# Rounding the joined high word of a float64 weight before its low bits are added

## The chip, the cores and the metric

The kernel runs on one core of a Trainium2 chip. The time is the device time of one execution in microseconds (us). The engines go by the names of the profile: PE is TensorE (PEld its weight loads), DVE is VectorE, ACT is ScalarE, POOL is GpSimd, SP issues the DMAs.

## The reference, cut to what matters

```python
def _attn_ref(q, k, v, n_sink, window):          # q, k, v: 4 x 8 x 768 x 64, float32
    scores = scale * np.matmul(q, k.transpose(0, 1, 3, 2))
    keep = is_sink | in_window                    # 4 sinks, a window of 128
    scores = np.where(keep, scores, -1000000000.0)
    ...
    return np.matmul(a, v).astype(np.float32)

def _moe_ref(x, w_in, w_out, s, b):               # x: 3072 x 512, w_in: 512 x 2048, w_out: 2048 x 512
    h = x @ w_in
    r = np.maximum(h, 0.0)
    g = s * (r * r) + b
    return (g @ w_out).astype(np.float32)
```

The attention's output is the x of the second function. Two lines of the set-up decide this case: `w_in` and `w_out` are float32 draws times a NumPy float64 scalar, so both arrive as float64, 8 bytes a number. The chip's engines take them as pairs of 32-bit words.

## The kernel before, in words

**The work in the large.** The 3072 tokens are eight chunks of 384. Each chunk has an attention part and a two-layer part (in the code `moe_steps`): `l1(f)` multiplies the chunk with columns f of `w_in` (line 598, 12 matmuls of 384 columns), and `l2(f)` adds g times rows f of `w_out` into three accumulators (line 617, 9 matmuls of 512 columns), for f from 0 to 15, l2 two steps behind l1. While the two-layer part of chunk c runs, the attention of chunk c+1 is put between its steps. Chunks 0 and 1 have a plain attention (class `Plain`): scores on PE (line 500), mask and maximum on DVE (515), the exponential on ACT (517), the division on DVE (`norm`, lines 522, 523 and six multiplications at 528), transposes on PE (540), their copies on ACT (542), the product with v on PE (551), and the result split in two on ACT and DVE (553, 554).

**Two words a weight.** A matmul here multiplies rounded float32 (F32R). Every operand is therefore held as a rounded part and a remainder, and each product is made of three matmuls (rounded x rounded, rounded x remainder, remainder x rounded). Sixteen weights f have to be made from float64 in that way, each a tile of 128 x 1024 numbers, and this is done once, for chunk 0. The scores and transposes of chunk 1 run in the same stretch.

**How one weight f is made.** `load_weight(f)` brings the float64 pairs into the place of weight f+1 (the tile w{f+1}); `raw[..., 0]` is the low word of each number, `raw[..., 1]` the high one. `make_weight(j)` has three steps for a weight, at j = 2f, 2f+1 and 2f+2:

- 211, ACT: the low word is scaled down to the 3 bits that the high word lacks; 212, ACT: the high word, read as a float32, is scaled so that its exponent fits.
- 213, DVE: the high word is shifted left by 3 into a scratch tile `wt`; 214, DVE: sign and shifted bits are joined, into the high word.
- 216, POOL: the low bits are added as integers, and the sum goes into the high word.
- 220, ACT: the sum is rounded into F32R, piece 0 of weight f (tile w{f}).
- 225: sum minus rounded part, the remainder, into piece 1. POOL does it for odd f, DVE for even f.

The last three raws (f = 13, 14, 15) come in halves or quarters with the same steps.

**What sets the order.** The instructions of an engine run in the order of its queue. That order is made when the kernel is built, by a scheduler that sorts the instructions of the whole program by when it reckons them ready; the kernel's own text gives only the start of it (`before(f)` asks, ahead of l1(f), for loads up to f + 6 and for the steps up to j = 2f + 4). Waits are semaphores between engines. So a changed dependency also moves instructions on the engines that take part, and those on either side of them.

**The WAR side.** Since raw f lies in the place of weight f+1, line 220 for weight f+1 must wait until line 225 for weight f has read its raw.

Of the kernel before, what the change touches and what calls it, by code (L numbers as in the profile page):

```python
# [6 lines left out]
F32 = mybir.dt.float32  # L7
# [5 lines left out]
ALU = mybir.AluOpType  # L13
# [27 lines left out]
def tile_kernel(ctx, tc, qT, kT, k0, v, vsk, n_sink, window, w, s, b, out):  # L41
    nc = tc.nc
# [127 lines left out]
    def place(f):  # L170
        return (const if f < NEARLY else late[0]).tile([P, 2, 2, DM], F32, tag=f"w{f}", name=f"w{f}")
# [15 lines left out]
    def scratch(f, j):  # L187

        if len(raws[f]) == 1:
            tag = f"w{NF - 2 + f % 2}"  # L190
            return (late[0] if late else first).tile([P, 2, DM], I32, tag=tag, name="wt", bufs=1)
        return wk.tile([P, DM], I32, tag="ot", name="wt")[:, :raws[f][j].shape[1]]

    def piece(f, j, t):

        n = len(raws[f])
        if n == 1:
            return weight[f][:, :, t, :]
        a = DM * 2 // n
        return weight[f][:, j * 2 // n, t, j * a % DM:j * a % DM + a]  # L200

    def make_weight(j):

        f = j // 2
        if j % 2 == 0 and f < NF:
            for i, raw in enumerate(raws[f]):
                lo, hi = raw[..., 0], raw[..., 1]
                t = scratch(f, i)  # L210
                nc.scalar.activation(lo, lo.bitcast(U32), AF.Copy, scale=2.0 ** -29)
                nc.scalar.mul(hi.bitcast(F32), hi.bitcast(F32), 2.0 ** -111)
                nc.vector.tensor_scalar(out=t, in0=hi, scalar1=3, scalar2=None, op0=ALU.logical_shift_left)  # L213
                nc.vector.scalar_tensor_tensor(out=hi, in0=hi, scalar=-0x80000000, in1=t,  # L214
                                               op0=ALU.bitwise_and, op1=ALU.bitwise_or)
                nc.gpsimd.tensor_tensor(out=hi, in0=hi, in1=lo, op=ALU.add)  # L216
        if j % 2 == 1:
            weight[f] = place(f).bitcast(F32R)
            for c, raw in enumerate(raws[f]):
                nc.scalar.copy(piece(f, c, 0), raw[..., 1].bitcast(F32))  # L220
        f -= 1
        if j % 2 == 0 and f >= 0:
            for c, raw in enumerate(raws[f]):
                e = nc.gpsimd if f % 2 == 1 else nc.vector
                e.tensor_tensor(out=piece(f, c, 1), in0=raw[..., 1].bitcast(F32), in1=piece(f, c, 0).bitcast(F32), op=ALU.subtract)
            raws.pop(f)


# [491 lines left out]
    def weights(n_load, n_make):  # L720
        while made[0] < min(n_make, 2 * NF + 1):
            while made[0] // 2 >= loaded[0] and loaded[0] < NF:
                load_weight(loaded[0])
                loaded[0] += 1
            make_weight(made[0])
            made[0] += 1

        n_wide = NF - NARROW - 1
        while loaded[0] < min(n_load, NF) and (loaded[0] < n_wide or made[0] > 2 * n_wide - 2):
            load_weight(loaded[0])  # L730
            loaded[0] += 1
# [102 lines left out]
```

## Time and profile before

| | |
|---|---|
| median of 3 executions | 739.83 us (738.43 to 743.51) |
| the profiled execution, its own time | 739.34 us |
| its span in the trace | 737.2 us |
| mean granted TensorE clock | 0.977 of 2.4 GHz |
| busy: PE, DVE, ACT, POOL | 704.9, 516.1, 480.0, 396.3 us |

A row of a timeline has the start in us, the duration, the engine, the line, the operation, the output and input tiles with their shapes (partitions x elements), the count, and in brackets the idle time of the engine before it with what ended that. Durations of consecutive instructions on DVE and ACT overlap by some 0.1 us. A row of waits names who waited for whom, the total, the number of times and the longest. A row by windows has, for a stretch of the span, the busy time of each engine with its instructions, then the granted clock, the DMA engines' share and GB/s.

### The profile page before, as it was taken

What the parts mean: (1) busy time and instruction counts of PE and PEld (TensorE: products, weight loads), DVE (VectorE), ACT (ScalarE), POOL (GpSimd) and SP (SyncE); (2) the same over time, 40 slices, a digit from 0 to 9 for tenths busy, and PEclk for the clock granted to TensorE, in tenths of its full rate; (3) what the DMA queues carried; (4) which work ended last, traced back from release to release, by engine and by line L of the source; (5) the groups of instructions that cost most, each with busy time, mean ns of one, the idle gap of its engine ahead of it and who ended that gap; (6) DMA issues with size and microseconds to landing.
All of it is one profiled execution on the core that took longest, in us unless ns stands there. A gap on an engine that the chain in (4) does not pass through costs nothing.

```text
span 737.2 us, 11878 instructions
## 1 busy us (share of the span) xinstructions
PE 704.9 (96%) x3848; PEld 622.0 (84%) x3848; DVE 516.1 (70%) x1213; ACT 480.0 (65%) x1169; POOL 396.3 (54%) x641
## 2 busy tenths in 40 slices
PE   6788899899999999999999999999999999999996
PEld 3367677789988999999998999999999999989895
DVE  6779999738984788757785588847886589743331
ACT  5978888568774787656884677746775677633222
POOL 2254555348991689616773589816775389710000
PEclk9879989999999999999999999999999999999998
DMA  7844122041210212111121222111111212000001
GB/s 280 337 171 193 33 102 72 15 139 51 80 63 31 84 55 65 34 61 54 46 64 44 82 63 64 46 54 49 56 53 45 84 42 59 12 18 26 1 1 47
DMA packets 27221, 53.01 MB, mean 72 GB/s; under 512 B 3472, under 2 KB 15376, under 8 KB 25232
## 3 DMA queue, kind: packets, MB, share of 16 engines
q1 hardware_dynamic: 27152, 52.18, 21.2%
q8 instruction: 32, 0.52, 0.3%
q14 instruction: 37, 0.30, 0.1%
HBM read 45.88 MB, written 6.29 MB: 71 GB/s over the span
## 4 chain that ended last, share of the span: by engine, by line
PE 79%; DVE 10%; DMA 3%; ACT 3%; POOL 2%; issue 1%; SPq 1%; POOLq 0%; ACTq 0%; DVEq 0%
PE po L617 32%; PE h L598 32%; PE o L376 3%; PE sc L303 2%; PE sc L304 2%; PE sc L324 2%; DMA vf<-in_v 2%; DMA w<-in_w 2%; DVE w L214 2%; DVE g L606 1%; DVE wt L213 1%; PE ts L390 1%; POOL w L216 1%; DVE smf L528 1%; DVE r L603 1%
## 5 line engine op out<-in xcount | busy, mean ns | idle before, releaser
L598 PE MATMUL h<-x,w 128*128 128x384 f32 x1536 | 299.8, 344 | 1.1 <-ACT tf L542 0.8
L617 PE MATMUL po<-w,g 128*128 128x512 f32 x1152 | 298.0, 404 | 0.0
L598 PEld LDWEIGHTS h<-x,w 128*128 128x128 f32 x1536 | 268.6, 189 | 6.7 <-ACT tf L542 1.1
L617 PEld LDWEIGHTS po<-w,g 128*128 128x128 f32 x1152 | 212.4, 191 | 45.0 <-issue 2.7
L603 DVE SCALAR_TENSOR_TENSOR r<-h,sb,r 128x384 f32<-128x384 f32 x128 | 78.6, 614 | 82.5 <-ACT r L601 82.2
L606 DVE SCALAR_TENSOR_TENSOR g<-r,sb,g 128x384 fp32r<-128x384 f32 x128 | 102.0, 797 | 39.0 <-ACT g L605 38.2
L340 POOL TENSOR_TENSOR hl<-two,hl 128x256 fp32r<-128x256 f32 x128 | 99.3, 776 | 21.4 <-ACT hl L339 18.2
L601 ACT ACTIVATE r<-h 128x384 f32<-128x384 f32 x128 | 62.3, 487 | 66.7 <-PE h L598 66.5
L605 ACT ACTIVATE g<-r,sb 128x384 fp32r<-128x384 f32 x128 | 78.7, 615 | 34.1 <-DVE r L603 32.8
L317 POOL TENSOR_TENSOR sm<-sm 128x128 f32<-128x128 f32 x128 | 68.0, 531 | 59.5 <-ACT sm L314 55.5
L314 ACT ACTIVATE sm<-sm,negm 128x272 f32<-128x272 f32 (+1 forms) x144 | 73.1, 507 | 35.4 <-DVE negm L308 31.0
L308 DVE CUSTOM_DVE_ANT_0 sm<-sc,msk 128x272 f32<-128x272 f32 (+1 forms) x144 | 60.4, 419 | 40.4 <-PE sc L304 32.6
L284 POOL TENSOR_TENSOR kl<-kraw,kh 128x544 fp32r<-128x544 f32 (+1 forms) x48 | 63.1, 1315 | 21.7 <-ACT kh L282 21.7
L339 ACT CAST hl<-two 128x256 fp32r<-128x256 f32 x128 | 50.6, 395 | 31.6 <-DVE two L337 31.6
L216 POOL TENSOR_TENSOR w<-w 128x1024 int32<-128x1024 int32 (+1 forms) x17 | 32.6, 1919 | 45.6 <-DVE w L214 25.1
L337 DVE TENSOR_TENSOR two<-sc,split 128x256 f32<-128x256 f32 x128 | 53.0, 417 | 4.4 <-POOL hl L340 4.2
L318 POOL COPY psk<-sm 128x48 f32<-128x48 f32 x144 | 40.7, 282 | 26.7 <-ACT sm L314 26.1
L289 POOL TENSOR_TENSOR vv<-vraw,vv 128x256 fp32r<-128x256 f32 (+1 forms) x48 | 34.4, 718 | 24.6 <-ACT vv L288 24.6
L376 PE MATMUL o<-hl,vv 128*128 128x256 f32 (+1 forms) x256 | 44.5, 276 | 0.0
L303 PE MATMUL sc<-kh,qs 128*128 128x272 f32 (+1 forms) x144 | 42.6, 298 | 0.0
L376 PEld LDWEIGHTS o<-hl,vv 128*128 128x128 f32 x256 | 39.6, 189 | 2.9
L304 PE MATMUL sc<-kl,qs 128*128 128x272 f32 (+1 forms) x144 | 41.3, 288 | 0.0
(129 smaller groups left out, 904.4 us busy)
## 6 DMA issues: line engine op xcount, KB each, us to landing
w<-in_w SPq DMA_DIRECT2D x15, 1024.0 KB, 9.0
kraw<-in_kT SPq DMA_DIRECT2D x32, 272.0 KB, 2.6
out<-ot SPq DMA_DIRECT2D x24, 256.0 KB, 2.0
qraw<-in_qT SPq DMA_DIRECT2D x24, 192.0 KB, 2.4
vraw<-in_v SPq DMA_DIRECT2D x16, 256.0 KB, 2.7
kraw<-in_kT SPq DMA_DIRECT2D x16, 208.0 KB, 2.4
vsraw<-in_vsk SPq DMA_DIRECT2D x24, 64.0 KB, 2.0
vraw<-in_v SPq DMA_DIRECT2D x8, 192.0 KB, 2.4
```

Of the source, the lines that this page charges most:

```text
L284: nc.gpsimd.tensor_tensor(out=hd.kl[:, :kw], in0=hd.k[:, :kw], in1=hd.kh[:, :kw].bitcast(F32), op=ALU.subtract)
L308: nc.vector.tensor_tensor_reduce(out=sm[:, :n], in0=sc[:, :n], in1=m, scale=-0.125, scalar=BIG, op0=ALU.add, op1=ALU.min, accum_out=negm[: ...
L314: nc.scalar.activation(sm[:, :n], sm[:, :n], AF.Exp, bias=negm[:, uu], scale=-1.0, accum_out=pp.zz[:, i, hh:hh + 1])
L317: nc.gpsimd.tensor_tensor(out=sm[:, c1:c1 + P], in0=sm[:, p1:p1 + P], in1=sm[:, c1:c1 + P], op=ALU.add)
L340: nc.gpsimd.tensor_tensor(out=lo, in0=both, in1=hi.bitcast(F32), op=ALU.subtract)
L376: nc.tensor.matmul(hd.o[:, q0:q0 + n * P], hd.vv[:, kb, :], hd.hl[:, t, c0 * P:(c0 + n) * P], start=(hd.n == 0), stop=(i == BLK - 1 and kb ...
L598: nc.tensor.matmul(h[:, :CH], weight[f][:, 0, wi, cc * P:(cc + 1) * P], x[xi][:, cc, :], start=(i == 0), stop=(i == 11))
L601: nc.scalar.activation(r, h[:, :CH], AF.Relu, scale=1.0 / WUP)
L603: nc.vector.scalar_tensor_tensor(out=r, in0=h[:, :CH], scalar=sw_ap, in1=r, op0=ALU.mult, op1=ALU.mult)
L605: nc.scalar.activation(gg[:, 0, :], r, AF.Identity, bias=b_ap, scale=1.0)
L606: nc.vector.scalar_tensor_tensor(out=gg[:, 1, :], in0=r, scalar=b_ap, in1=gg[:, 0, :].bitcast(F32), op0=ALU.add, op1=ALU.subtract)
L617: nc.tensor.matmul(po[tb], gg[:, gi, tsl], weight[f][:, 1, wi, :], start=(f == 0 and i == 0), stop=(f == NF - 1 and i == 2))
```

## The change

The integer addition on POOL puts its sum into the low word instead of the high one, so that the high word stays as DVE joined it. ACT's rounding (line 220, not touched in the text) then reads the high word without the low bits, and the remainder (line 225) is taken from the sum in the low word. The rounded part can so be made of a number whose three lowest bits are zero; rounded part plus remainder is the sum, as before.

```diff
-                nc.gpsimd.tensor_tensor(out=hi, in0=hi, in1=lo, op=ALU.add)
+                nc.gpsimd.tensor_tensor(out=lo, in0=hi, in1=lo, op=ALU.add)
...
-                e.tensor_tensor(out=piece(f, c, 1), in0=raw[..., 1].bitcast(F32), in1=piece(f, c, 0).bitcast(F32), op=ALU.subtract)
+                e.tensor_tensor(out=piece(f, c, 1), in0=raw[..., 0].bitcast(F32), in1=piece(f, c, 0).bitcast(F32), op=ALU.subtract)
```

Line 220 depended on 216 and now depends on 214. Line 225 depended on 220 and now depends on 220 and 216. The numbers and sizes of the instructions stay. PE's queue changes in 13 rows out of 2459 (one score matmul earlier), POOL's in 10 rows at the end of the stretch, SP's not at all. DVE's and ACT's queues change through the whole stretch in which weights are made.

On DVE, at the middle of the stretch (trace of before: 79 to 95 us). In these names w9_604 is the raw of weight 8 in the place of weight 9, w8_828 is weight 8, w10_651 the raw of weight 9; sc is a bank of scores, smf their exponentials, zf the divisors, g and r belong to l1.

```order
 L213 TENSOR_SCALAR wt_774<-w9_604 128x1024
-L214 SCALAR_TENSOR_TENSOR w9_604<-w9_604,wt_774 128x1024
 L606 SCALAR_TENSOR_TENSOR g_738<-r_735,sb_72,g_738 128x384
 L515 ISA smf_766,negm_102<-sc_762,m_all_70 128x384
 L515 ISA negm_102 128x1
+L214 SCALAR_TENSOR_TENSOR w9_604<-w9_604,wt_774 128x1024
 L515 ISA smf_769,negm_102<-sc_764,m_all_70 128x384
 L515 ISA negm_102 128x1
-L213 TENSOR_SCALAR wt_830<-w10_651 128x1024
-L214 SCALAR_TENSOR_TENSOR w10_651<-w10_651,wt_830 128x1024
+L225 TENSOR_TENSOR w8_828<-w9_604,w8_828 128x2x512
 L603 SCALAR_TENSOR_TENSOR r_796<-h_783,sb_72,r_796 128x384
```

The join of raw 8 stands two scores later than before, the remainder of weight 8 stands right behind the last score, and the two DVE steps of raw 9 have moved behind it.

On DVE, at the end of the stretch (trace of before: 127 to 132 us). w15_1013 is the raw of weight 14 in halves, w14_1193 is weight 14, the wraw tiles are the quarters of raw 15.

```order
 L214 SCALAR_TENSOR_TENSOR wraw_1015<-wraw_1015,wt_1196 128x256
 L214 SCALAR_TENSOR_TENSOR wraw_1017<-wraw_1017,wt_1202 128x256
+L225 TENSOR_TENSOR w14_1193<-w15_1013,w14_1193 128x512 x2
 L213 TENSOR_SCALAR wt_1208<-wraw_1019 128x256
-L225 TENSOR_TENSOR w14_1193<-w15_1013,w14_1193 128x512
+L213 TENSOR_SCALAR wt_1214<-wraw_1021 128x256
 L214 SCALAR_TENSOR_TENSOR wraw_1019<-wraw_1019,wt_1208 128x256
-L225 TENSOR_TENSOR w14_1193<-w15_1013,w14_1193 128x512
-L213 TENSOR_SCALAR wt_1214<-wraw_1021 128x256
 L214 SCALAR_TENSOR_TENSOR wraw_1021<-wraw_1021,wt_1214 128x256
```

Both remainders of weight 14 now stand ahead of the last two quarters of raw 15.

On ACT, near 64 us of the trace of before. w5_642 is weight 5, w6_402 its raw, g_622 and r_666 belong to l1(3) and l1(4), w8_552 is raw 7, w6_711 weight 6.

```order
 L212 ACTIVATE w7_404<-w7_404 128x1024
+L220 CAST w5_642<-w6_402 128x2x512
+L605 ACTIVATE g_622<-r_619,sb_72 128x384
 L211 ACTIVATE w8_552<-w8_552 128x1024
-L605 ACTIVATE g_622<-r_619,sb_72 128x384
-L220 CAST w5_642<-w6_402 128x2x512
 L601 ACTIVATE r_666<-h_653 128x384
 L542 COPY tf_672<-tp_673 128x2x2x128
 L212 ACTIVATE w8_552<-w8_552 128x1024
```

The rounding of weight 5 has moved two instructions forward.

## Rows read from the trace of the kernel before

**Rows 1.** The page, part 4: the chain that ended last, by engine.
```profile
PE 79%; DVE 10%; DMA 3%; ACT 3%; POOL 2%; issue 1%; SPq 1%; POOLq 0%; ACTq 0%; DVEq 0%
```

**Rows 2.** By windows: the weight stretch, the two after it.
```profile
50.00:132.00 82.00, 71.25 (x360) 57.05 (x361) 78.77 (x136) 66.20 (x129) 43.90 (x25) 0.94 0.30 113
132.00:160.00 28.00, 28.00 (x150) 23.99 (x147) 14.31 (x34) 15.05 (x35) 8.17 (x12) 0.94 0.26 84
160.00:737.20 577.20, 569.65 (x3164) 520.90 (x3162) 387.28 (x919) 363.59 (x927) 328.09 (x578) 1.00 0.16 50
```

**Rows 3.** Waits of PE, then of ACT, 45 to 140 us.
```profile
PE tp L540 <- DVE smf L528: 7.4, 3, 2.9
PE o L551 <- ACT tf L542: 2.5, 2, 1.9
PE h L598 <- ACT tf L542: 0.8, 1, 0.8
...
ACT w L220 <- POOL w L216: 4.8, 6, 1.6
```

**Rows 4.** Timeline of DVE: lines 528 and 606 alone, then beside POOL.
```profile
16.57 1.65 DVE L528 TENSOR_SCALAR sm<-sm,zf 128x128 f32<-128x128 f32 x6
...
59.39 0.61 DVE L606 SCALAR_TENSOR_TENSOR g<-r,sb,g 128x384 fp32r<-128x384 f32 x1
...
64.17 2.65 DVE L528 TENSOR_SCALAR smf<-smf,zf 128x256 f32<-128x256 f32 x4
...
67.99 3.35 DVE L214 SCALAR_TENSOR_TENSOR w<-w,wt 128x1024 int32<-128x1024 int32 x1
...
76.64 0.61 DVE L603 SCALAR_TENSOR_TENSOR r<-h,sb,r 128x384 f32<-128x384 f32 x1
...
80.22 2.77 DVE L606 SCALAR_TENSOR_TENSOR g<-r,sb,g 128x384 fp32r<-128x384 f32 x1
```

**Rows 5.** Timeline of POOL in the same stretch.
```profile
63.86 1.89 POOL L216 TENSOR_TENSOR w<-w 128x1024 int32<-128x1024 int32 x1 [5.28 <-ACT r L601]
67.00 3.25 POOL L225 TENSOR_TENSOR w<-w,w 128x1024 fp32r<-128x1024 f32 x1 [1.24 <-ACT w L220]
...
75.72 2.75 POOL L216 TENSOR_TENSOR w<-w 128x1024 int32<-128x1024 int32 x1 [2.42 <-DVE w L214]
79.75 2.83 POOL L225 TENSOR_TENSOR w<-w,w 128x1024 fp32r<-128x1024 f32 x1 [1.27 <-ACT w L220]
82.54 2.21 POOL L216 TENSOR_TENSOR w<-w 128x1024 int32<-128x1024 int32 x1
...
91.03 2.41 POOL L225 TENSOR_TENSOR w<-w,w 128x1024 fp32r<-128x1024 f32 x1 [2.45 <-ACT w L220]
```

**Rows 6.** Timeline of PE: where it waited for DVE, the matmuls behind.
```profile
66.55 0.66 PE L540 MATMUL tp<-identr,smf 128*128 128x128 f32 x3 [2.49 <-DVE smf L528]
...
68.10 3.79 PE L617 MATMUL po<-w,g 128*128 128x512 f32 x9
...
93.98 0.90 PE L540 MATMUL tp<-identr,smf 128*128 128x128 f32 x3 [2.90 <-DVE smf L528]
...
131.40 1.61 PE L551 MATMUL o<-tf,vf 128*64 128x384 f32 x12 [1.95 <-ACT tf L542]
...
138.68 2.25 PE L617 MATMUL po<-w,g 128*128 128x512 f32 x9
```

**Rows 7.** Timeline of DVE, 90 to 95 us and 113 to 131 us.
```profile
90.41 3.85 DVE L528 TENSOR_SCALAR smf<-smf,zf 128x128 f32<-128x128 f32 x6
...
113.89 1.22 DVE L225 TENSOR_TENSOR w<-w,w 128x1024 fp32r<-128x1024 f32 x1
...
129.33 0.41 DVE L214 SCALAR_TENSOR_TENSOR wraw<-wraw,wt 128x256 int32<-128x256 int32 x1
129.67 0.68 DVE L225 TENSOR_TENSOR w<-w,w 128x512 fp32r<-128x512 f32 x1
```

**Rows 8.** Timeline of ACT at the end of the stretch.
```profile
130.44 0.43 ACT L220 CAST w<-wraw 128x256 fp32r<-128x256 f32 x1 [1.75 <-DVE w L225]
```

## The prediction, made before the kernel ran

> **What bounds the kernel now.** I read the chain that ended last first [rows 1]: PE has 79% of it, DVE 10%, ACT and POOL together 5%. Next the windows [rows 2]. From 160 us to the end PE is busy 569.65 of 577.20 us, and no weight is made there: that stretch can only be shifted as a whole. The change sits in 50 to 132 us (the sixteen weights and the attention of chunk 1). There PE is busy 71.25 of 82 us, DVE 78.77, ACT 66.20, POOL 43.90. So DVE is the engine that never rests, and PE waits: 7.4 us in three waits for the divisions at line 528, 2.5 and 0.8 us for the transposes' copies on ACT [rows 3]. All of PE's idle time there is 82.00 - 71.25 = 10.8 us. That is the most that a shorter weight path could give, apart from the slower matmuls behind a wait (next part but one).
>
> The reader should then look at how long DVE's instructions take [rows 4]. Six divisions alone last 1.65 us, a line 606 alone 0.61. At 64.17 four divisions last 2.65, at 67.99 a join lasts 3.35, at 80.22 a line 606 lasts 2.77. POOL has an instruction under way in each case, and DVE's ends its own length after POOL's [rows 5]: 80.22 + 2.77 = 82.99, POOL's subtraction at 79.75 ends at 82.58. In the other direction POOL's addition at 75.72 lasts 2.75 instead of 1.89. Line 603, which reads PSUM, runs through at 0.61 us beside that addition. So DVE's work between tiles in SBUF and POOL's work exclude each other, whoever comes first, and part of DVE's 78.77 us is standing still. The Trainium skill has this in "SBUF — State Buffer", Who interferes with whom: DVE with two SBUF inputs or in a two-port mode and a GpSimd instruction take turns on one pair of ports, and the second to issue blocks fully. The trace agrees (2.77 against 0.61 us).
>
> **The change part by part.** *Work.* The 21 additions, 21 roundings, 21 remainders and the 42 DVE steps before them are the same number and size before and after. Cost of the work itself: 0. POOL's total hold is 43.90 us either way.
>
> *What is removed.* ACT no longer waits for POOL's addition: 4.8 us in six waits [rows 3]. ACT is busy 66 of 82 us, so most of that was slack; it is on the path only where a line 605 or a copy for PE stood behind the rounding. Bounds: 0 and -4.8. I take 0 but for the end (below), since DVE, with 78.77 of 82, goes on setting the pace.
>
> *What is brought forward.* POOL's remainder of an odd weight began about 1.25 us after the addition, because it waited for the rounding (idle 1.24 at 67.00, 1.27 at 79.75 [rows 5]). Now the rounding is done beside the addition, and the remainder follows on its heels. It is no gain in itself: POOL idles almost half of the stretch. But it closes the gap in which DVE got through. How two POOL instructions back to back treat DVE is seen at 82.54: the addition queued there lasts 2.21 instead of 1.89, and in those 0.3 us line 606 of DVE ran. One DVE instruction gets in between, not a group.
>
> Place one, 63 to 71 us. Before: the addition of raw 6 ends at 65.75, all four divisions run until 66.75, then comes the remainder at 67.00, and PE starts its transposes at 66.55 [rows 4 to 6]. After: addition, one division, remainder (some 2.4 us, as at 91.03), three divisions. The last one ends some 2.4 us later, plus about 0.8 us for lateness from the weights before (an estimate: a third of one collision like the join's, 3.35 against 1.22 in line 214 elsewhere). PE: +3.3. DVE gets most of it back, since the join at 67.99 no longer meets the remainder: +1.0 at its end.
>
> Place two, 79 to 95 us. Line 605 now stands ahead of the rounding on ACT, so line 606 at 80.22 is spared its 2.2 us. The join of raw 8, which stands one score later, meets POOL's remainder in its stead: +2.4. Then the remainder of weight 8 on DVE, directly behind the last score, waits for its addition: 1.9 us less one score (I put it at 0.5, a little under line 603's 0.61) = +1.4. Queued behind it are line 603 and line 554. The two DVE steps of raw 9 come after them, so raw 9's addition and POOL's remainder fall upon the six divisions: 1.65 + 1.9 + 2.4 = 5.9 us instead of the 3.85 at 90.41 [rows 7]. With 0.6 us of lateness at their start, the last division ends some 2.8 us later, and PE, which waits for it at 93.98 [rows 6], is 2.8 us late from there.
>
> Place three, 95 to 115 us. The order changes back and forth (a shift moves behind a score, a remainder ahead of a join). By my working DVE catches up to about 0 at 104 us and loses it again in the next pair on POOL: the remainder of weight 12, which ended at 115.0 before [rows 7], ends at 117.5. PE is not held by it.
>
> Place four, the end. The second half of weight 14's remainder ran at 129.67 behind a join of 0.41 us and a shift that I put at 0.7, like the remainder's own 0.68 [rows 7]; both now stand behind it: -1.1. ACT's rounding of weight 15 waited 1.75 us for just this remainder [rows 8], behind it stands the transposes' copy, and PE waited 1.95 us for that at 131.40. So the copy comes 2.5 - 1.1 = 1.4 us later than before. PE's own 2.8 us disappear in its waits there (0.8 and 1.95 us). Net: +1.4 us at 131 us, and the rest of the span is shifted by it.
>
> *The rule against the trace.* The same section of the Trainium skill says that ScalarE has ports of its own and that issue order decides who blocks. By it, moving the rounding is free and the closer pair on POOL costs what I have summed. Were the two engines independent, only the -1.1 at the end would be left, near 738.
>
> *Sum.* 739.34 (the profiled execution, 2.1 us of it outside the span) + 1.4 = 740.7. The median is 0.5 above the profiled one; I say 741.
>
> **The rivals.** *The waits were on the path.* If ACT's 4.8 us sat in front of lines 605 and 606 everywhere, the stretch shortens by them: 739.3 - 4.8 = 734.5. For it: the waits are directly ahead of such instructions at the end. Against it: DVE idles only 3 us in the 82. To be faster by over 1% (7.4 us, about what a measurement of this kernel can tell from no change) it would also need most of PE's remaining 6 us of waiting.
>
> *The pair on POOL splits the divisions, and PE pays twice.* One mechanism, at places one and two: PE is 3.3 and 2.8 us late, and behind each longer wait its matmuls run slower. Behind the 2.49 us wait nine of them took 3.79 us, against 2.25 at 138.68 [rows 6]: +1.5 each time. If nothing of it is absorbed later: 739.3 + 3.3 + 2.8 + 3.0 = 748.4. It decides once the divisions are split at both places and PE, not DVE, is what is late at 131 us. Against it: after both waits PE already ran slow before, and its waits further on (0.8 and 1.95 us) absorb some.
>
> *Hidden anyway.* DVE's remainders need POOL's sum just as before, and DVE's total is the same: 739.3, no change.
>
> **How the numbers follow.** The forecast and its neighbourhood, 737 to 744: 0.45. Hidden anyway, 738 to 741, which is the same answer: 0.20. Waits on the path, about 734.5: 0.17, of which 0.04 falls beyond -1%. PE pays twice, about 748: 0.18, half of it beyond +1%. So faster 0.04, within 1% 0.87, slower 0.09. The bounds of the unknown costs are 734.5 and 748.4; the range 735 to 747 leaves out the outer part of each.
>
> **What would show it right or wrong.** Right: ACT's waits for line 216 are gone; POOL's odd remainders start directly after the additions; the four divisions near 64 us and the six near 90 last 4 us or more; DVE gets a new wait for line 216 ahead of weight 8's remainder; the wait at 131 us for the copy is shorter in itself. DVE's busy time in the stretch stays within 2 us. Wrong: DVE's busy time there falls by 4 us or more (fewer collisions: the first rival), or PE's waits for line 528 grow from 7.4 to over 14 us and are not given back (the second).

## The result, and the profile after

The changed kernel takes 742.93 us (median of 7 runs, 742.25 to 745.34) beside 739.33 us for the kernel before (7 runs, 736.28 to 743.51): ratio 1.0053, 95% interval 1.0028 to 1.0077. Timed a second time (below, `f5_after_again`) the ratio was 1.0042, 1.0021 to 1.0062. The change makes the kernel 3 to 4 us slower. The forecast was 741.0, within 1% and on the slow side; the loss, 3.6 us in the first timing and 2.9 in the second, is two to two and a half times the 1.4 us that I had worked out.

The same three windows as [rows 2]. The profiled execution is the slowest of the seven (745.34 us), and it began late: its first expert matmul (L598) starts at 50.45 us, that of the kernel before at 45.29. So a fixed window does not hold the same work in both, and the 4.1 us by which DVE's busy time falls from 78.77 says little. Cut at events that both profiles have (A to D, next section), DVE's 174 instructions are busy for 99.37 us before and 98.61 now.

```profile
50.00:132.00 82.00, 70.12 (x348) 56.08 (x345) 74.64 (x127) 64.57 (x118) 38.02 (x20) 0.90 0.33 122
132.00:160.00 28.00, 28.00 (x148) 22.80 (x147) 17.84 (x39) 16.38 (x38) 11.05 (x12) 0.96 0.20 58
160.00:737.20 577.20, 576.44 (x3204) 527.43 (x3202) 391.06 (x929) 367.26 (x938) 330.64 (x584) 1.00 0.17 51
```

PE's waits from 45 to 145 us, to be laid beside [rows 3]. That for the divisions (L528) has grown from 7.4 to 9.7 us, that for the copies (L542) has shrunk from 3.3 to 0.7, and one for line 603 is new. ACT has no wait for POOL's addition (line 216) left, where there were 4.8 us; its rounding now waits for DVE's join (line 214) instead, 5.4 us in three (last row, ACT from 45 to 140 us).

```profile
PE tp L540 <- DVE smf L528: 9.7, 3, 5.0
PE h L598 <- DVE r L603: 2.1, 1, 2.1
PE o L551 <- ACT tf L542: 0.7, 1, 0.7
...
ACT w L220 <- DVE w L214: 5.4, 3, 2.7
```

DVE's timeline, the counterpart of [rows 4] and [rows 7] (start, duration, instruction; in brackets the wait before it):

```profile
69.95 4.87 DVE L528 TENSOR_SCALAR smf<-smf,zf 128x256 f32<-128x256 f32 x4
...
86.87 3.02 DVE L214 SCALAR_TENSOR_TENSOR w<-w,wt 128x1024 int32<-128x1024 int32 x1
...
91.89 1.23 DVE L225 TENSOR_TENSOR w<-w,w 128x1024 fp32r<-128x1024 f32 x1 [1.53 <-POOL w L216]
...
96.42 5.50 DVE L528 TENSOR_SCALAR smf<-smf,zf 128x128 f32<-128x128 f32 x6
...
129.27 0.61 DVE L603 SCALAR_TENSOR_TENSOR r<-h,sb,r 128x384 f32<-128x384 f32 x1
```

POOL beside it, the counterpart of [rows 5]. The remainder (L225) stands 0.08 us behind the addition (L216) at place one and 0.34 us behind it at place two, where there were 1.25 us and more. The reader should add up: 71.61 + 2.40 = 74.01, and only then do the last divisions of the 4.87 us get through.

```profile
69.64 1.89 POOL L216 TENSOR_TENSOR w<-w 128x1024 int32<-128x1024 int32 x1 [5.37 <-ACT r L601]
71.61 2.40 POOL L225 TENSOR_TENSOR w<-w,w 128x1024 fp32r<-128x1024 f32 x1
...
96.64 2.01 POOL L216 TENSOR_TENSOR w<-w 128x1024 int32<-128x1024 int32 x1 [4.79 <-ACT w L212]
98.99 2.40 POOL L225 TENSOR_TENSOR w<-w,w 128x1024 fp32r<-128x1024 f32 x1 [0.34 <-ACT w L220]
```

PE's timeline, the counterpart of [rows 6]. The waits of 2.49 and 2.90 us have become 4.99 and 4.50. At 139.49 the wait of 1.95 us for the copy is gone, and at 129.93 stands the new one.

```profile
74.55 0.90 PE L540 MATMUL tp<-identr,smf 128*128 128x128 f32 x3 [4.99 <-DVE smf L528]
...
101.66 0.90 PE L540 MATMUL tp<-identr,smf 128*128 128x128 f32 x3 [4.50 <-DVE smf L528]
...
129.93 3.71 PE L598 MATMUL h<-x,w 128*128 128x384 f32 x12 [2.09 <-DVE r L603]
...
139.49 1.52 PE L551 MATMUL o<-tf,vf 128*64 128x384 f32 x12
```

### The profile page after: what moved, and what is told of

Read it like the earlier page. It is cut to its first block, busy times and chain, and to the rows that moved or that the text cites. A ratio compares the mean times of both kernels' runs of the same rounds, so it can differ in the third digit from the quotient of the medians.

```text
span 743.2 us, 11899 instructions
## 1 busy us (share of the span) xinstructions
PE 708.1 (95%) x3848; PEld 625.8 (84%) x3848; DVE 515.8 (69%) x1213; ACT 480.6 (65%) x1169; POOL 393.5 (53%) x641
## 4 chain that ended last, share of the span: by engine, by line
PE 79%; DVE 4%; ACT 2%; POOL 1%; issue 1%; POOLq 0%; ACTq 0%
PE h L598 33%; PE po L617 32%; PE o L376 3%; PE sc L303 2%; PE sc L304 2%; PE sc L324 2%; PE ts L390 1%; DVE w L214 1%; PE o L368 1%; DVE smf L528 1%; PE os L399 1%; DVE r L603 1%; PE zb L406 0%; DVE wt L213 0%; PE o L551 0%
## 5 line engine op out<-in xcount | busy, mean ns | idle before, releaser
L598 PE MATMUL h<-x,w 128*128 128x384 f32 x1536 | 301.1, 345 | 2.3 <-DVE r L603 2.1
L598 PEld LDWEIGHTS h<-x,w 128*128 128x128 f32 x1536 | 269.8, 190 | 8.3 <-DVE r L603 2.5
L606 DVE SCALAR_TENSOR_TENSOR g<-r,sb,g 128x384 fp32r<-128x384 f32 x128 | 97.7, 764 | 38.2 <-ACT g L605 37.4
L216 POOL TENSOR_TENSOR w<-w 128x1024 int32<-128x1024 int32 (+1 forms) x17 | 30.8, 1816 | 62.8 <-DVE w L214 31.9
L318 POOL COPY psk<-sm 128x48 f32<-128x48 f32 x144 | 40.6, 282 | 26.7 <-ACT sm L314 26.0
L303 PE MATMUL sc<-kh,qs 128*128 128x272 f32 (+1 forms) x144 | 42.6, 298 | 0.0
L283 DVE TENSOR_TENSOR qs<-qraw,qs 64x384 fp32r<-64x384 f32 x48 | 38.5, 803 | 4.1 <-ACT qs L279 2.7
```

What stands on the lines that cost most here:

```text
L598: nc.tensor.matmul(h[:, :CH], weight[f][:, 0, wi, cc * P:(cc + 1) * P], x[xi][:, cc, :], start=(i == 0), stop=(i == 11))
L606: nc.vector.scalar_tensor_tensor(out=gg[:, 1, :], in0=r, scalar=b_ap, in1=gg[:, 0, :].bitcast(F32), op0=ALU.add, op1=ALU.subtract)
```

## The experiments

**How they are read.** Executions of one kernel differ by some 6 us (the kernel before ran from 736 to 743 us in each of the comparisons), and the first profile of the changed kernel began its experts 5 us later than the one before. So I cut each profile at four events that every kernel has: A, the start of the last six divisions of chunk 0 (35 to 42 us; the work at weight 1); B, the start of chunk 1's four divisions (place one of the forecast); C, the start of its six (place two); D, the first score of the next stage (L303). From D to the end it is 582 to 583 us everywhere. All times in us, from the timelines; the ratio is against the kernel before on the same chip. The divisions of `f8_div_on_act` run on another engine, so it has no line.

```
kernel                       A     A-B    B-C    C-D    A-D    ratio (95%)
before                     36.87  27.30  26.24   63.8  117.3
e1_sum_low                 37.88  27.46  26.24   62.3  116.0   0.9983 (0.9960-1.0005)
g10_before_rem1            37.92  26.53  26.24   62.3  115.1   1.0000 (0.9984-1.0017)
g11_before_rem159          37.11  26.54  26.23   62.1  114.9   0.9991 (0.9971-1.0012)
e4_before_both             35.16  28.64  26.17   64.1  118.9   1.0005 (0.9983-1.0027)
after                      41.57  28.38  26.47   64.4  119.2   1.0053 (1.0028-1.0077)
f5_after_again             37.66  28.78  26.70   64.4  119.8   1.0042 (1.0021-1.0062)
h12_rem3_shift             35.35  29.13  26.68   64.4  120.2   1.0051 (1.0033-1.0069)
g9_rem59_behind            36.49  29.09  25.57   65.1  119.7   1.0024 (1.0007-1.0041)
f7_rem5_behind             35.68  29.24  25.57   63.5  118.3   1.0026 (1.0003-1.0048)
f6_rem1_behind             37.31  26.14  25.94   64.3  116.4   1.0012 (0.9990-1.0034)
e2_rem_behind              39.25  26.12  25.56   63.9  115.6   1.0005 (0.9982-1.0028)
e3_both_behind             35.32  27.67  26.23   63.2  117.1   0.9989 (0.9964-1.0013)
```

In several of them an instruction "waits for the last division". That is one more dependency; by the traces the order on every engine stays that of the kernel which the run starts from, except in e4 (see there). It is made by

```
divided, sync = [], mybir.DependencyInfo(mybir.DependencyClass.Sync, mybir.DependencyReason.DATA)
def behind(ins):
    tc.add_manual_dep(ins.ins, divided[-1].ins.name, sync, reason="behind the divisions")
```

with every division (L528) appended to `divided` when it is issued.

**The place of the sum alone: e1_sum_low.** The changed kernel, but the rounding reads the sum in the low word, so it waits for POOL's addition as before, and the order on every engine is that of the kernel before.

```
-                nc.scalar.copy(piece(f, c, 0), raw[..., 1].bitcast(F32))
+                nc.scalar.copy(piece(f, c, 0), raw[..., 0].bitcast(F32))
```

> The sum goes into the low word, as in the change, but ScalarE rounds the sum, so that the chain addition, rounding, remainder and the order of all instructions are those of the kernel before. Theory (the loss comes from the freed rounding: GpSimd's pairs back to back and VectorE's moved remainders): as before, 739.3 +-1.5, PE's waits for the divisions (line 528) near 7.4 us. Rival (the place of the sum, or a start that happens to be slower, makes the loss): near 742.9.

Measured: 738.34 us, ratio 0.9983 (0.9960 to 1.0005), and PE's waits for the divisions as before:

```profile
PE tp L540 <- DVE smf L528: 7.4, 3, 2.9
```

Where the sum is put costs nothing. The loss comes from the freed rounding, that is from the order and the moments that follow from it. This run is also a second sample of the old order: its C to D is 62.3 us, as in `g10` and `g11`, so the 63.8 of the first profile is at the upper end. The 1.5 us between them are one place: behind PE's wait of 1.95 us the nine matmuls of line 617 took 3.79 us in the first profile (granted clock 0.58) and 2.35 in e1 behind 1.96 us (1.00).

**The loss undone: e2_rem_behind.** The changed kernel; POOL's remainders of weights 1, 5 and 9 wait for the last division.

```
-                e.tensor_tensor(out=piece(f, c, 1), ...)
+                behind(e.tensor_tensor(out=piece(f, c, 1), ...)) if f in (1, 5, 9) else e.tensor_tensor(out=piece(f, c, 1), ...)
```

> The change, in its own order on every engine, with one wait more: GpSimd's remainders of weights 1, 5 and 9 wait for the last of the divisions that they used to cut in two. Theory: the three groups of divisions end some 2.4 us earlier, PE's waits for line 528 fall from 9.7 us (45 to 145 us) to under 6, the time falls by 2 to 5 us, to 738 to 741. Rival (VectorE's remainders that wait for GpSimd's sum, and the queue moved behind them, make the loss): the waits of line 225 on VectorE stay at 4 us or more, and the time stays within 1 us of 742.9.

Measured: 739.86 us, ratio 1.0005 (0.9982 to 1.0028). The three groups of divisions last 1.67, 2.65 and 3.29 us instead of 3.65, 4.87 and 5.50 (first of them chunk 0's):

```profile
39.25 1.67 DVE L528 TENSOR_SCALAR sm<-sm,zf 128x128 f32<-128x128 f32 x6
...
65.37 2.65 DVE L528 TENSOR_SCALAR smf<-smf,zf 128x256 f32<-128x256 f32 x4
...
90.93 3.29 DVE L528 TENSOR_SCALAR smf<-smf,zf 128x128 f32<-128x128 f32 x6
```

PE's waits for line 528 fall to 6.6 us, not under 6, and line 225's waits on DVE for POOL's addition rise from 2.1 to 4.1 us: the rival's sign came, its time did not. So most of the loss hangs on the remainders' moment, with the new orders in place. But the run undoes three places at once, and one of them, chunk 0's at 39 us, is not among those of my forecast. Nor does it repair the whole way: C to D stays 1.6 us above e1, and A to B and B to C become shorter than in the kernel before. Its fair partner is g11 (below), the old order with the same three waits: 1.0005 against 0.9991, with intervals that overlap.

**The additions held back too: e3_both_behind and e4_before_both.** As e2, and the additions of weights 1, 5 and 9 wait as well (those of 5 and 9 are issued in their odd step, in front of the rounding); once on the changed kernel, once on the kernel before.

```
+                behind(nc.gpsimd.tensor_tensor(out=lo, in0=hi, in1=lo, op=ALU.add))          # f == 1
...
+            [behind(nc.gpsimd.tensor_tensor(out=raw[..., 0], in0=raw[..., 1], in1=raw[..., 0], op=ALU.add)) for raw in raws[f] if f in (5, 9)]
```

> As the run before, and the additions of raws 1, 5 and 9 wait for the same divisions too (the order of every engine is again that of the change). Theory: the groups of six divisions last about 1.7 us and the four about 1.0 (3.65, 5.50 and 4.87 in the change), the first matmul of the two-layer part starts 3 to 4 us earlier from the same start, the whole is 735 to 738, faster than the kernel before. Rival (weights are late then, since GpSimd's work is only put off): PE waits for a weight in line 598 instead, and the time is 741 or more.

> The kernel before, in its order, with the same additions and remainders of raws and weights 1, 5 and 9 behind the divisions. Theory (divisions cut by GpSimd are what PE waits for in either kernel): 735 to 737; the gain over the kernel before is smaller than that of the run before over the change, by 1 to 3 us. Rival: the chain through ScalarE is longer here, so late weights cost more: 739 or more.

Measured: 739.36 us (0.9989, 0.9964 to 1.0013) and 740.29 us (1.0005, 0.9983 to 1.0027). The gain that I expected did not come. In e4 the later place of two additions also gave POOL, DVE and ACT another order, so it is not the kernel before "in its order". The divisions were free of POOL (1.67, 1.26 and 1.66 us in both kernels), but DVE's next instructions met what had been pushed behind, and weights came late. PE's two longest waits of e4 from 40 to 145 us:

```profile
PE h L598 <- POOL w L225: 6.2, 3, 3.2
PE tp L540 <- DVE smf L528: 2.5, 2, 1.9
```

**A second profile of the change: f5_after_again.** No edit.

> The changed kernel once more, beside the kernel before on one chip. Stage = from the first L598 to the first L303 in the profile: 108.9 us before, 110.3 in the first profile of the changed kernel. If the 3.6 us between the first medians were 1.4 of the stage and the rest a late start by chance, this median lies within 2 us of the kernel before, the stage is 109.5 to 111.5 and the first L598 begins before 48 us (it began at 50.5 in the first profile). If the change itself delays the start, the median is again 3 us or more longer and the first L598 again begins near 50.

Measured: 741.50 us, 2.9 above the kernel before in that comparison, and the first L598 at 46.54 us. So neither of the two statements is right as a whole: the late start of the first profile was chance, as the first says, and the loss is there all the same. The table shows where: 1.1 and 1.5 us from A to B, 0.2 and 0.5 from B to C, and from C to D 0.6 against the first profile of the old order or 2.1 against the three others. Together 3.2 to 3.8 us against e1, which is near what the medians say (3.6 and 2.9), and 1.9 to 2.5 against the first profile of the old order. About a third of the 3.2 to 3.8 lies ahead of place one (0.9 to 1.3 us against e1), where my forecast had nothing, and more than half from C to D. DVE's busy time and waits from A to B, before (36.87 to 64.17) and then in f5 (37.66 to 66.44); columns as in [rows 2]:

```profile
36.87:64.17 27.30, 24.82 (x115) 19.40 (x115) 22.98 (x41) 20.96 (x36) 11.94 (x6) 0.81 0.55 214
```

```profile
DVE wt L213 <- PE o L551: 2.5, 1, 2.5
DVE r L603 <- ACT r L601: 0.9, 1, 0.9
DVE g L606 <- ACT g L605: 0.9, 1, 0.9
```

```profile
37.66:66.44 28.78, 25.25 (x115) 19.68 (x115) 24.20 (x41) 20.30 (x35) 10.95 (x6) 0.82 0.54 211
```

```profile
DVE w L225 <- ACT w L220: 2.3, 1, 2.3
DVE smf L515 <- PE sc L500: 1.7, 1, 1.7
DVE wt L213 <- ACT w L212: 0.5, 1, 0.5
```

The same 41 instructions of DVE take 24.20 instead of 22.98 us: that is 1.2 of the 1.5 us. Most of it stands at POOL's addition and remainder of weight 3: the shift (line 213) there lasts 1.58 us instead of 0.69, the line 606 behind it 2.80 instead of 2.39. DVE's waits are others than before, but their sum grows only from 4.3 to 4.6 us. One of them is 1.7 us for PE's scores, for which DVE did not wait before. DVE comes to them sooner in its new order, and PE's transposes, which begin 2.4 us after A instead of 0.4, end 5.45 us after it instead of 4.98. Before, four of the six divisions were done when POOL's remainder of weight 1 started at 37.81; now it starts at 37.45, ahead of all six, and holds the first of them until 39.93. DVE's timeline of the kernel before, then of the changed one:

```profile
36.87 1.01 DVE L528 TENSOR_SCALAR sm<-sm,zf 128x128 f32<-128x128 f32 x4
```

```profile
37.66 2.27 DVE L528 TENSOR_SCALAR sm<-sm,zf 128x128 f32<-128x128 f32 x1
```

**One place at a time: f6_rem1_behind, f7_rem5_behind, g9_rem59_behind.** As e2, with `f == 1`, with `f == 5`, and with `f in (5, 9)`.

> The changed kernel, only GpSimd's remainder of weight 1 waits for the last division in issue. It tells the two places apart. My theory: the four divisions near 65 us last about 2.65 us again (4.9 with the change), the six near 91 us stay at 5 or more, and the stage (first L598 to first L303) falls by no more than 1 us from the changed kernel's 110.3, since PE's lateness at place one is partly taken up again at place two. Rival, that place one alone made the loss: the stage is 109 or less and the median that of the kernel before.

> The changed kernel, only GpSimd's remainder of weight 5 waits for the last division. My theory: the four near 65 us last 4.5 or more, the six near 91 us about 3.3 instead of 5.5, and the stage falls by 0.5 to 1.5 us from 110.3. Rival, that place two is covered by waits behind it: stage unchanged at 110.3.

> The changed kernel, GpSimd's remainders of weights 5 and 9 wait for the last division, that of weight 1 does not: the counterpart of the run that held back weight 1 alone. Theory, that the larger part of the loss lies at weight 1 (near 37 us, ahead of what I forecast): from the start of chunk 0's last six divisions to chunk 1's four divisions it is 28.4 to 29.3 us as in the changed kernel (27.3 before), from these to the first L303 some 89.3 (90.0 before, 90.8 with the change), and the median lies 1 to 2.5 us above the kernel before. Rival, that the two places I forecast carry the loss: the median is within 0.7 us of the kernel before.

Measured: 739.61 us (1.0012, 0.9990 to 1.0034), 741.03 us (1.0026, 1.0003 to 1.0048) and 741.34 us (1.0024, 1.0007 to 1.0041). g9 has both forecast places repaired:

```profile
36.49 3.83 DVE L528 TENSOR_SCALAR sm<-sm,zf 128x128 f32<-128x128 f32 x6
...
65.58 2.65 DVE L528 TENSOR_SCALAR smf<-smf,zf 128x256 f32<-128x256 f32 x4
...
91.15 3.29 DVE L528 TENSOR_SCALAR smf<-smf,zf 128x128 f32<-128x128 f32 x6
```

and the interval of its time stays above the kernel before (from 1.0007); B to C falls by 1.1 us, A to B stays at 29.1. From B to the first L303 it is 90.7 us, where I had expected 89.3: no less than with the change (90.8). f6 has both places of the forecast as bad as the change made them (4.87 and 5.48 us), and only chunk 0's divisions free:

```profile
37.31 1.67 DVE L528 TENSOR_SCALAR sm<-sm,zf 128x128 f32<-128x128 f32 x6
...
63.45 4.87 DVE L528 TENSOR_SCALAR smf<-smf,zf 128x256 f32<-128x256 f32 x4
```

and A to B falls from 28.8 to 26.1 us. Its whole list of DVE's waits from 37 to 64 us is one line; that for the scores is gone:

```profile
DVE w L225 <- POOL w L216: 2.0, 1, 2.0
```

In the profiles weight 1's remainder is worth 2.6 us from A to B, and place one is worth 1.1 from B to C. For place two no profile shows a gain: C to D is 65.1 us in g9, which spares its six divisions, and 63.5 in f7, which does not. The intervals of f6, f7 and g9 overlap, so the times alone would not order the three. The stretches do for A to B: it is 28.4 to 29.2 us in the five profiles of the changed order that leave weight 1's remainder alone, and 26.1 in f6 and e2, which hold it back.

The expectations of f6 and f7 were aimed at the wrong places: the remainder of weight 5 is the one of place one, that of weight 1 lies ahead of it. So f6 left the four divisions at 4.87 us (I had expected 2.65), and f7 brought the four to 2.65 and left the six at 5.43 (expected: 4.5 or more and 3.3). In f6 I had expected the stage from L598 to L303 to fall by at most 1 us from 110.3; it grew to 110.8, since L598 starts earlier there (42.90) than the rest can follow. In f7 it fell by 1.0 to 109.3, the number that I expected, but at place one instead of place two.

**The same wait in the kernel before: g10_before_rem1, g11_before_rem159.** The kernel before has a collision at weight 1 too (divisions of 3.81 us). Edit as in f6 and e2, on the kernel before.

> The kernel before, its remainder of weight 1 on GpSimd waits for the last division of chunk 0; orders and places of the sums as before. The kernel before has a collision there too (divisions of 3.8 us). If the wait is worth something by itself and did not only undo the change, the six divisions last 1.7 us, the first L598 comes some 1.5 to 2.8 us sooner behind them, the 27.3 us to the four divisions become 26.1, and the median falls by 0.5 to 1.5 us. Rival: VectorE loses to the late remainder what PE gains (its next shift lasts 2.7 instead of 0.7 us), 27.3 stay, and the median stays within 0.5 us.

> The kernel before, its remainders of weights 1, 5 and 9 all wait for the last division of their time. If each is worth something beside the change: the six divisions near 90 last 3.3 instead of 3.85 us, and the median lies 0.5 to 2 us below the kernel before, the best of all runs. Rival: same as the kernel before within 0.5 us, since VectorE is busy all the time and only the order of its instructions is paid for.

Measured: 738.60 us (1.0000, 0.9984 to 1.0017) and 738.11 us (0.9991, 0.9971 to 1.0012). A to B is 0.8 us shorter, and no gain shows in the time. In g11 the six divisions near 90 us last 1.67 us (3.3 expected), and that brings nothing either. So of the 2.6 us that f6 wins back from A to B, 1.5 are what the change cost there (28.78 - 27.30), and the rest is not the change's loss but a gain that the old order had open as well. g11 has the lowest median of its comparison and the shortest way from A to D, but no run here is shown to be faster than the kernel before.

**Is it the closed pair as such? h12_rem3_shift.** Weight 3's addition and remainder stand back to back too (between A and B), and DVE's line 606 lasts 2.80 us there. The remainder waits for DVE's shift of weight 4, so that one DVE instruction more gets in between.

```
-                nc.vector.tensor_scalar(out=t, in0=hi, scalar1=3, scalar2=None, op0=ALU.logical_shift_left)
+                divided.append(nc.vector.tensor_scalar(out=t, in0=hi, scalar1=3, scalar2=None, op0=ALU.logical_shift_left))
...
-                e.tensor_tensor(out=piece(f, c, 1), ...)
+                behind(e.tensor_tensor(out=piece(f, c, 1), ...)) if f == 3 else e.tensor_tensor(out=piece(f, c, 1), ...)
```

> The changed kernel, only GpSimd's remainder of weight 3 waits, for VectorE's shift of weight 4 (L213), so that one more VectorE instruction gets through between it and the addition of weight 3. It tells two parts of the 28.4 to 28.8 us between the last divisions of chunk 0 and the four of chunk 1 apart (27.3 before). If the closed pair of weight 3 is what costs there, the L606 behind the shift lasts about 0.6 instead of 2.8 us and the stretch falls to 27.0 to 28.0, the median to within 2 us of the kernel before. Rival, that the lateness comes from weight 1's pair alone and a block spared here is paid by the next VectorE instruction (the join L214): L606 is short, L214 lasts about 2.5 instead of 1.2, the stretch stays at 28.3 or more, and the median 2 to 3.5 us above the kernel before.

Measured: 742.06 us (1.0051, 1.0033 to 1.0069), A to B 29.1 us: what the rival said came. DVE's timeline of the changed kernel (f5), then that of h12:

```profile
53.35 1.58 DVE L213 TENSOR_SCALAR wt<-w 128x1024 int32<-128x1024 int32 x1
54.86 2.80 DVE L606 SCALAR_TENSOR_TENSOR g<-r,sb,g 128x384 fp32r<-128x384 f32 x1
57.59 1.21 DVE L214 SCALAR_TENSOR_TENSOR w<-w,wt 128x1024 int32<-128x1024 int32 x1
```

```profile
51.34 1.59 DVE L213 TENSOR_SCALAR wt<-w 128x1024 int32<-128x1024 int32 x1
52.85 0.61 DVE L606 SCALAR_TENSOR_TENSOR g<-r,sb,g 128x384 fp32r<-128x384 f32 x1
53.38 3.46 DVE L214 SCALAR_TENSOR_TENSOR w<-w,wt 128x1024 int32<-128x1024 int32 x1
```

Line 606 wins 2.80 - 0.61 = 2.19 us, and the join behind it loses 3.46 - 1.21 = 2.25. The block is handed on to the next instruction in full. So the run does not tell what weight 3's pair costs: it moved the block and did not make it smaller. In f6 the block moves too, from the six divisions (1.67 us instead of 3.65) to the shift behind them (2.74 instead of 0.68), and DVE is busy for 24.01 us from A to B, as in f5 with 24.20. But PE, which waits for the divisions and not for the shift, ends its transposes 3.47 us after A where f5 has 5.45, and DVE's waits sum to 26.14 - 24.01 = 2.1 us where f5 has 28.78 - 24.20 = 4.6. I take it that this is what matters: whether PE waits for the instruction that is hit.

**The divisions on another engine: f8_div_on_act.** The changed kernel, all divisions on ScalarE.

```
-                    nc.vector.tensor_scalar(out=sm, in0=sm, scalar1=pp.z[:, 0, i, hh:hh + 1], scalar2=None, op0=ALU.mult)
+                    nc.scalar.mul(sm, sm, pp.z[:, 0, i, hh:hh + 1])
```

> The changed kernel with all divisions (L528) on ScalarE, which GpSimd does not hold up, and which loses no time to it in any row. If PE's waits for L528 (9.7 us in three) are what the change made longer, they fall below 4 us in sum, VectorE's busy time in the stretch falls by about 9 us, and the time is 1 to 4 us below the kernel before. Rival, that ScalarE itself is then late: its six divisions are some 3 us in its queue ahead of copies for PE, PE then waits for these, and the time stays within 1 us of the changed kernel.

Measured: 749.54 us, ratio 1.0144 (1.0112 to 1.0177), worse than either theory said. PE's waits for chunk 1's divisions are gone, but from 45 to 165 us PE waits for weights and gates instead:

```profile
PE h L598 <- POOL w L225: 7.2, 4, 2.6
PE po L617 <- DVE g L606: 4.9, 2, 2.7
PE o L551 <- ACT tf L542: 3.2, 1, 3.2
```

Six divisions last 2.5 us on ACT against 1.65 on DVE [rows 4], and ACT's roundings and squares stand behind them; the first L598 starts at 51.0 us. ACT was busy 66 of 82 us before [rows 2]; that it had no room on its queue at these moments is my reading. The scheduler also gave DVE, ACT and PE another order in this run, and what that did is not told apart from the move. That PE waits for the divisions was not a reason that they could leave DVE.

## Why the prediction was right or wrong

**Right: what the removed wait is worth.** I took ACT's 4.8 us at 0, and the rival that they were on the path (734.5) is out: the waits for the addition are gone, the rounding waits for DVE's join instead (5.4 us), and the time rose.

**Right: the mechanism and its marks.** POOL's remainders of weights 1, 3, 5 and 9 follow the addition within 0.34 us (that of weight 7 not: it starts 1.70 us behind), and DVE's divisions are split. I had put the last of the four 3.2 us later and the last of the six 2.8; counted from the first L598 they end 2.84 and 2.5 us later. I had put the six at 5.9 us; they last 5.50. Weight 8's remainder got its new wait for line 216, 1.53 us against my 1.4. As the Trainium skill has it in "SBUF — State Buffer", Who interferes with whom, the one that issues second blocks fully; h12 agrees, with 2.19 us won and 2.25 lost. One sign came out as wrong by its letter: DVE's busy time from 50 to 132 us fell by 4.1 us. That is the late start; from A to D it fell by 0.8. Three small workings do not come out and change nothing: a third of the join's collision is 0.7 us, not 0.8; place two adds up to 5.9 - 3.85 + 0.6 = 2.65, not 2.8; and the line 606 at 80.22 ends 0.41 us after POOL's instruction, not its own length of 0.61.

**Right in kind: most of PE's lateness at places one and two is given back.** At place one PE's transposes come 2.84 us later (from the first L598), but B to C grows by only 0.2 to 0.5 us; sparing the place (f7, g9) brings B to C down to 25.57 us, where the changed kernel has 26.5 and 26.7. That is also why the rival in which PE pays twice (748.4) did not come true. What place two costs in the end these runs do not show.

**Wrong: the stretch ahead of place one is missing from the sum.** I had put the change into 50 to 132 us, "the sixteen weights", and the working begins at 63 us. But weight 1's remainder stands at 37.81 in the trace of before, and where in the group of six divisions it would now fall was not asked. It falls ahead of the first division (behind the first in f7, g9 and h12) instead of behind the fourth, the join of weight 3 now stands behind the scores, for which DVE waits, and A to B grows by 1.1 and 1.5 us. f6 holds that remainder back and wins 2.6 us; g9 spares both places that I had named and keeps the loss. By DVE's rows most of the 1.5 us stands at weight 3's pair (1.58 and 2.80 us); but f6 has that pair just so (1.58 and 2.81) and is shorter, so it is not the cause by itself. How the 1.5 us divide between the late scores and that pair was not tried.

**Wrong: "PE is not held by it" and "PE's own 2.8 us disappear in its waits there".** This was places three and four. The copy came 1.5 us later counted from C (138.27 - 96.42 = 41.85 against 130.76 - 90.41 = 40.35), where I had worked out 2.5 - 1.1 = 1.4. But PE did not wait for it any more. It was held earlier, for 2.09 us at 129.93, by line 603, which now stands behind two joins of half weights where it stood behind one. And the twelve matmuls behind that wait took 3.71 us at a granted clock of 0.59, most of it at the lower of the two levels (1.2 of 2.4 GHz), where those at 120.78 before took 2.38 at 1.00. These rows are of the changed kernel (the wait's stretch) and of the kernel before:

```profile
129.93:133.64 3.71, 3.71 (x13) 3.62 (x14) 3.71 (x12) 2.20 (x7) 3.08 (x4) 0.59 0.00 0
```

```profile
120.78:123.16 2.38, 2.38 (x13) 2.20 (x14) 2.38 (x6) 0.84 (x2) 1.42 (x2) 1.00 0.00 0
```

So the net of 1.4 us at the end was near the 0.6 to 2.1 measured from C to D by luck: the way was another than mine. That part of the loss is argued from these rows; no run took the wait for line 603 away. But all eight profiles in the changed kernel's order have this wait, 2.0 to 3.0 us, and none of the four in the old order (the kernel before, e1, g10, g11). C to D is 64.1 us in the mean of the eight (63.2 to 65.1) and 62.6 in that of the four, whichever remainders are held back. The clock is a part of it that comes and goes: in f7 the matmuls behind the same wait took 2.37 us (granted clock 1.00), and C to D is 63.5.

```profile
123.76 2.37 PE L598 MATMUL h<-x,w 128*128 128x384 f32 x12 [2.66 <-DVE r L603]
```

**Sum.** Forecast 1.4 us, all of it from the end. Measured 3.2 to 3.8 against the old order's e1: 0.9 to 1.3 from A to B, 0.2 to 0.5 from B to C, 2.1 from C to D. The first is shown by f6 and g9, the last and largest is argued.

## What to carry to other kernels

A wait that "costs nothing" on an idle engine can be what spaces two instructions of another engine apart; when it is removed, look at every place where that pair now falls, from the first one on, and ask which instruction of the blocked engine is next and who waits for that one. When two engines block each other in full, moving the block saves nothing by itself (2.19 us won, 2.25 lost); it can pay where the instruction that is spared has a waiter and the one that is hit has none, as from A to B in f6; in g10 even that brought no time that could be measured. And cut profiles at events, not at times: here the start of the work differed by 6 us between profiles of the same order.

## What was not expected of the hardware

A DVE instruction of 6 columns is held like one of 1024: line 522 (128x6), 0.17 us alone, lasts 1.86 us in the changed kernel's second profile, because it starts at 35.53 while POOL's addition of weight 1 runs until 34.63 + 2.73 = 37.36.

```profile
35.53 1.86 DVE L522 TENSOR_SCALAR zf<-zf 128x6 f32<-128x6 f32 x1
```

And the start is not the same from one execution to the next: with the same instructions in the same order up to event A it came at 41.57 us in the first profile of the changed kernel and at 35.68 in `f7`. The granted clock differs just there: 0.78 and 0.73 in the one, 1.00 and 1.00 in the other, in the windows below (the column in front of the last two). What sets it was not tried.

```profile
0.00:20.00 20.00, 13.03 (x55) 7.36 (x57) 11.99 (x71) 9.58 (x30) 4.77 (x22) 0.78 0.74 280
20.00:35.00 15.00, 13.08 (x67) 7.84 (x69) 8.23 (x32) 13.14 (x30) 1.93 (x2) 0.73 0.95 383
```

```profile
0.00:20.00 20.00, 13.93 (x74) 6.93 (x76) 12.35 (x72) 11.82 (x33) 4.82 (x22) 1.00 0.79 284
20.00:35.00 15.00, 9.14 (x64) 5.04 (x62) 12.87 (x40) 15.00 (x38) 4.25 (x2) 1.00 0.94 378
```
